# Low halves of split fp32 operands placed 128 bytes further on, modulo 256, than their high halves

## The chip, the core and the metric

The kernel runs on one core of a Trainium2 chip. Its time is the device time of one execution in microseconds (us); the figure for a kernel is the median of its runs. A profile is one further execution that the hardware profiler recorded; its span runs from the first to the last recorded instruction. TensorE (PE in the rows) does the matrix products, and its loads of the stationary operand are shown as an engine of their own, PEld. VectorE is DVE, ScalarE is ACT, GpSimd is POOL, and SP is the engine whose queue issues the DMAs.

## What is computed

Block-causal attention, then two multilayer perceptrons, all in float32 (2304 tokens, 8 heads of 64, model width 512, inner width 2048):

```python
# attention: q, k, v are (4, 8, 576, 64); query block i sees key blocks j <= i, blocks of 64
scores = np.where(mask, scale * (q @ k.T), -1e9)
x = (exp(scores - max) / (sum + 1e-9)) @ v        # -> (2304, 512)
h = x @ w1_in;  x = (h * np.cos(h)) @ w1_out      # first MLP
h = x @ w2_in;  r = np.maximum(h, 0.0)
out = (r * r) @ w2_out                            # second MLP
```

## The kernel before

**Split products.** TensorE runs the MLPs on float32 operands rounded to its short float32 form (`F32R`). To keep precision, each operand is a pair: a high half (the rounded value) and a low half (what rounding left). `hi_part` and `lo_part` make them, on ScalarE, VectorE or GpSimd. One product of pairs is three matmuls into the same PSUM bank (`mm3`, lines 903 to 907):

```python
matmul(ps, lh, rh, first, False, holds)
matmul(ps, lh, rl, False, False, holds)
matmul(ps, ll, rh, False, last, holds)
```

The first operand is stationary (128 columns, loaded into the array by an LDWEIGHTS of its own), the second one moves through it (256, 320 or 512 columns). All matmuls of this sort stand on line 548 in the profile.

**Stages.** From 0 to some 405 us the attention runs, with half of the first MLP's inner width beside it as filler for TensorE: tiles `xs1`, `xs2` (256 and 320 tokens of one batch) move through `w` into `h` banks (`h_banks`), `h * cos(h)` is split into `g` tiles (`gh0` to `gh3` high, `gl0` to `gl3` low), and these move through `w` into `y` banks (`out_T`). From 405 to 590 us the other half of the first MLP runs on blocks of 512 tokens. Its first product is done with seven block products instead of eight: `load_quarters` makes seven forms of x (`x0` to `x6`) out of sums of its quarters, `x_parts` splits each into a high and a low half in one tile (`x_tile`), and `quad` runs the seven products, 12 matmuls each, against seven forms of the weights. From 590 to 800 us the second MLP's first half runs in the same manner; its second product has g stationary and `w` moving, 512 columns. From 800 us the other half of the second MLP runs, both its products with seven forms (`g_forms`, `right_factors`, `out_quad`).

In that second-MLP stage the forms of x are also written to DRAM (`keep`, tensor `xp_d`) and read back in the last stage (`kept_parts`).

**Order.** Every operation is recorded and put into a fixed order by a planner before anything is issued; tiles get their addresses from pools that are opened one after the other. `shim` puts a few bytes between pools, so that tiles begin at chosen places.

**Places modulo 256 bytes.** In the built program every stationary `w` tile of the pool `wa` begins at 0 modulo 256, and every one of the pool `wo` at 128. Every form of x, `xs` and `g`, high and low half alike, begins at 64. In the three stages from 405 us on, the weights of the first product lie in `wo` for one half of the inner columns (`c = 0` in the stage's loop) and in `wa` for the other (`c = 1`), so TensorE goes from one place to the other where the planned order changes `c`: from `wa` to `wo` at 520.5 and 641.7 us, from `wo` to `wa` at 840.0 us. In the last stage some forms of g and of the right-hand weights take the places of other tiles (`ws`, `t`, `c`, `n`, `x`, `raw`, `so`): there both operands of a product can begin at 64 modulo 128. In the attention's scores `kh` begins at 0 and `kl` at 128; the tiles `tail` begin at 0. The slice of 288 columns (1152 bytes) that their second product takes moves each start on by 128.

Of the kernel before, what the change touches and what calls it, by code (L numbers as in the profile page):

```python
# [2 lines left out]

# [8 lines left out]
F32R = mybir.dt.float32r  # L12
# [6 lines left out]
PSUM = bass.MemoryType.PSUM  # L19
# [37 lines left out]
class View:  # L57
    def __init__(self, vt, chain, ix, halves):
        self.vt, self.chain, self.ix, self.halves = vt, chain, ix, halves
# [34 lines left out]


class VTile(View):
    def __init__(self, pool, shape, dtype, tag, bufs, whole=False):
        self.pool, self.shape, self.dtype, self.tag, self.bufs = pool, shape, dtype, tag, bufs
        self.whole = whole
        n = int(np.prod(shape[1:]))  # L100
        self.grain = 32 if n >= 32 else 1
        self.full = (1 << (2 * (n // self.grain + 1))) - 1
        self.real = None
        self.users = []
        self.bank = self.banks = self.before = None
        super().__init__(self, [], np.arange(n).reshape(shape[1:]), 3)

    def alloc(self):
        if self.real is None:
            tag = self.tag if self.bank is None else f"bank{self.bank}"  # L110
            self.real = self.pool().tile(self.shape, self.dtype, tag=tag, name=self.tag, bufs=self.bufs)


class Banks:
# [30 lines left out]
class Recorder:  # L145
# [20 lines left out]
        self.kind = None  # L166
        self.phase = 0

    def tile(self, pool, shape, dtype, tag, bufs=1, whole=False):
        return VTile(pool, shape, dtype, tag, bufs, whole)  # L170

    @contextmanager
    def of(self, kind):
# [199 lines left out]
def f(v):  # L373
    return v.bitcast(F32)


def real(v):
    return v.ap() if isinstance(v, View) else v
# [3 lines left out]
def kernel(  # L382
# [18 lines left out]
    KD = DM // 128  # L401
    HALF = DFF // 256
# [5 lines left out]
    R = Recorder()  # L408


    def of(kind):
        def wrap(fn):
            def run(*args, **kw):
                with R.of(kind):
                    return fn(*args, **kw)

            return run

        return wrap
# [40 lines left out]
    def hi_part(hi, x):  # L460
        n = hi.size
        flexible(
            "hi",
            {
                "POOL": (
                    "POOL", n * 0.836 + 160,
                    lambda: nc.gpsimd.tensor_scalar(real(hi), real(x), 1.0, 1.0, op0=ALU.mult, op1=ALU.mult),  # L467
                ),
                "DVE": (
                    "DVE", n / 1.92 + 68, lambda: nc.vector.tensor_scalar(real(hi), real(x), 1.0, None, op0=ALU.mult), 2,  # L470
                ),
                "ACT": ("ACT", n / 1.2 + 92, lambda: nc.scalar.activation(real(hi), real(x), ACTF.Copy)),  # L472
            },
            [hi], [x],
        )

    def lo_part(lo, x, hi):
        n = lo.size
        if psum(x):
            return tt(lo, x, f(hi), ALU.subtract)  # L480
        flexible(
            "lo",
            {
                "POOL": (
                    "POOL", n * 2.1 + 350,
                    lambda: nc.gpsimd.tensor_tensor(real(lo), real(x), real(f(hi)), op=ALU.subtract), 1,
                ),
                "DVE": (
                    "DVE", n / 0.96 + 68,
                    lambda: nc.vector.tensor_tensor(real(lo), real(x), real(f(hi)), op=ALU.subtract), 1,  # L490
                ),
            },
            [lo], [x, hi],
        )
# [76 lines left out]
    def dma(out, in_, size, service=None):  # L571
        R.op(
            "DMA", max(400.0, size / 360.0), lambda: nc.sync.dma_start(out=real(out), in_=real(in_)), [out], [in_],
            lat=1250,
        ).service = size / 420.0 if service is None else service
# [5 lines left out]
    class Pool:  # L581


        def __init__(self, name, **kw):
            self.name, self.kw, self.pool, self.after, self.stack = name, kw, None, (), None
# [10 lines left out]
    def opened(stack, *names, **kw):  # L596
        got = []
        for n in names:
            p = Pool(n, **kw)
            p.open(stack)  # L600
            got.append(p)
        return got

    def later(names, **kw):
        return [Pool(n, **kw) for n in names]

    def shim(stack, name, n, **kw):

        if n:
            p = stack.enter_context(tc.tile_pool(name=name, bufs=1, **kw))  # L610
            p.tile([128, n // 4], F32, tag=name, name=name)
# [19 lines left out]
    shim(ctx, "shim1", 32)  # L631
    (wa_p,) = opened(ctx, "wa")
    shim(ctx, "shim2", 64)
    cv, st_p, g_p, o_p = opened(ctx, "cv", "st", "g", "o")
    shim(ctx, "shim3", 96, side="right")
    (psum_p,) = opened(ctx, "ps", space=PSUM)
    banks = Banks(8, *BANKS)
    xs_p, tmp = opened(s1, "xs1", "tmp1")
    (sb,) = opened(att, "att", side="right")

    def T(pool, shape, dtype, tag, bufs=1):
        return R.tile(pool, shape, dtype, tag, bufs, whole=pool.kw.get("space") == PSUM)

    x_d = T(dram, [KD, 128, NT], F32, "x_d")
    y1_d = T(dram, [KD, 128, NT], F32, "y1_d")
    y_d = T(dram, [KD, 128, NT], F32, "y_d")


# [27 lines left out]
    for i in range(2):  # L676
# [3 lines left out]
        whole = T(sb, [128, 128], F32, f"whole{i}")  # L680
# [531 lines left out]
    xs = {}  # L1212

    @of("split")
    def split_x(u, r):

        o, n = GROUPS[r - 1]
        if (u.b, r) not in xs:
            xs[u.b, r] = [T(xs_p, [128, KD, n], F32R, f"xs{r}{i}") for i in "hl"]
        hi, lo = xs[u.b, r]  # L1220
        hi_part(hi[:, u.p], u.xt[:, o:o + n])
        lo_part(lo[:, u.p], u.xt[:, o:o + n], hi[:, u.p])


    def new_g():
        return [[T(g_p, [128, 2, 512], F32R, f"g{i}{m}") for m in range(HALF // 2)] for i in "hl"]

    def row(g, m):
        return g[m // 2][:, m % 2]
# [1 line left out]
    def first_in(b, r):  # L1231
        g = new_g()
        in_cos(tmp, w1i, xs[b, r], g, GROUPS[r - 1][1], TOGETHER if (b, r) == (0, 1) else 1)
        return g
# [12 lines left out]
    def attend(i):  # L1247
        u = attention(i)
        for r in (1, 2) if u.part == 0 else (u.part,):
            split_x(u, r)  # L1250
# [15 lines left out]
    for group, steps in WORK:  # L1266
        R.phase = 0 if group == (0, 1) else 1 + group[0]
        g = first_in(*group)
# [4 lines left out]
        if group in ((0, 2), (1, 1)):  # L1273
            c = group[0]
            left_weights(w1_in, 2 + c, wi_d[c])
        if group in ((1, 2), (2, 1)):
            c = group[0] - 1
            staged_weights(row_chunks(w1_out, 2 + c, 3 + c), wo_d[c:c + 1])
        if group == (3, 1):
            wo_p, x3_p = later(("wo", "x3"), side="right")  # L1280
# [9 lines left out]
    def raw_rows(src, c0, n):  # L1290
# [5 lines left out]
            raw.append(t)  # L1296
        return raw

    def x_tile(j):
        return T(x3_p, [128, 2, 2, 256], F32R, f"x{j}")  # L1300

    def x_parts(forms, keep):

        ops = {}
        for j, x in forms:
            t = x_tile(j)
            hi, lo = t[:, 0], t[:, 1]
            hi_part(hi, x)
            lo_part(lo, x, hi)
            if keep is not None:  # L1310
                dma(keep[j], f(t).rearrange("p j k c -> p (j k c)"), 524288)
            ops[j] = hi, lo
        return ops

    @of("forms")
    def kept_parts(keep, which):

        ops = {}
        for j in which:
            t = x_tile(j)  # L1320
            dma(f(t).rearrange("p j k c -> p (j k c)"), keep[j], 524288)
            ops[j] = t[:, 0], t[:, 1]
        return ops

    @of("forms")
    def load_plain(src, c0, keep=None):

        x1, x2 = raw_rows(src, c0, 256)
        d = T(tmp3, [128, 2, 256], F32, "t0")
        add(d, x2, x1, ALU.subtract)  # L1330
        return x_parts(((0, x1), (1, x2), (4, d)), keep)
# [104 lines left out]
    def g_forms():  # L1436

        small = [(st_p, f"ws{i}", 1) for i in range(2)] + [(cv, "t", 2)] * 2 + [(cv, "c", 3)] * 3
        small += [(tmp3, "n", 1)] + [(tmp3, f"t{i}", 1) for i in range(4)]
        large = [(g_p, f"g{i}{m}", 1) for i in "hl" for m in range(HALF // 2)]  # L1440
        got = [{}, {}]
        for c in range(2):
            for i in (0, 3, 4, 5, 6, 1, 2):
                if small:
                    got[c][i] = [T(pool, [128, 2, 256], F32R, tag, n) for pool, tag, n in (small.pop(0), small.pop(0))]
                else:
                    pool, tag, n = large.pop(0)
                    t = T(pool, [128, 2, 2, 256], F32R, tag, n)
                    got[c][i] = [t[:, j] for j in range(2)]
        return got  # L1450
# [86 lines left out]
    for stage in range(3):  # L1537
# [4 lines left out]
        for turn_, i in enumerate(ROUNDS[stage]):  # L1542
# [3 lines left out]
            if stage < 2:  # L1546
                xs = (load_quarters if i < 4 else load_plain)(src, c0, xp_d[i] if stage and turn_ < 4 else None)
                g = new_g()
            else:
                if turn_:  # L1550
                    xs = kept_parts(xp_d[i], FIRST if i < 4 else (0, 1, 4))
                g = g_forms()
# [27 lines left out]
            if stage < 2 and 0 < turn_ < 3:  # L1580
                c = 2 * stage + turn_ - 1
# [61 lines left out]
```

## Time and profile before

| | |
|---|---|
| median of 3 runs | 973.34 us (973.02 to 973.65) |
| profiled execution, its own time | 974.84 us |
| its span | 973.0 us |
| PE busy | 951.8 us, 98% of the span, 6996 matmuls |
| PEld busy | 856.1 us, 88% |
| DVE busy | 713.8 us, 73% |
| ACT busy | 602.3 us, 62% |
| POOL busy | 208.3 us, 21% |

The granted TensorE clock (`PEclk`) stands at full speed from 72 us to the end. A matmul's recorded duration holds the way through the array and overlaps that of the next, so it says little; what a matmul costs in a stream is the time from its start to the next one's start. The chain of work that ended last gives this: a row of it that reads "10.88 PE h L548 x96" is 96 matmuls in a row that together moved the chain on by 10.88 us, 113.3 ns each.

### The profile page before, as it was taken

Reading aid. Unit: us, or ns where it says so; the run is one execution under the profiler, and the core shown is the slowest. Engines: PE = TensorE matmul, PEld = TensorE weight load, DVE = VectorE, ACT = ScalarE, POOL = GpSimd, SP = SyncE. Lnnn points to the kernel's source line nnn. Section 1 sums busy time; section 2 is a strip of 40 time slices with the busy share of each in tenths; the row PEclk is TensorE's granted clock in tenths of the full one; section 3 lists DMA queues with packets and bytes.
Section 4 is the critical chain, followed back from the end, with each engine's and each line's share of the span. In section 5 each row is a group of like instructions: output and inputs, shape, how many; then the busy total and the mean of one; then the engine's idle time right before and its main releaser. Section 6 shows DMA issues by size and latency. Waiting matters only on the chain.

```text
span 973.0 us, 19283 instructions
## 1 busy us (share of the span) xinstructions
PE 951.8 (98%) x6996; PEld 856.1 (88%) x6996; DVE 713.8 (73%) x1581; ACT 602.3 (62%) x1285; POOL 208.3 (21%) x313
## 2 busy tenths in 40 slices
PE   7979999999999999999999999999999999999998
PEld 5757987889898989999989889998898899999998
DVE  5898667687877455588879797987885737659565
ACT  5787588785889575484758476767564433324222
POOL 3554243447687781000000000000000000000000
PEclk8999999999999999999999999999999999999999
DMA  6755233355656347563355899796947779535321
GB/s 184 192 150 124 67 85 84 105 153 182 176 174 206 109 134 263 200 254 93 109 173 181 317 360 327 268 352 215 358 139 240 245 256 416 194 104 195 96 73 60
DMA packets 155150, 185.29 MB, mean 190 GB/s; under 512 B 71728, under 2 KB 119856, under 8 KB 155056
## 3 DMA queue, kind: packets, MB, share of 16 engines
q1 hardware_dynamic: 155056, 184.07, 57.5%
q8 instruction: 55, 0.90, 0.4%
q14 instruction: 39, 0.32, 0.1%
HBM read 114.29 MB, written 69.73 MB: 189 GB/s over the span
## 4 chain that ended last, share of the span: by engine, by line
PE 88%; DMA 5%; DVE 3%; ACT 2%; issue 1%; POOL 1%; SPq 0%; ACTq 0%; POOLq 0%; DVEq 0%
PE y L548 37%; PE h L548 34%; PE t L566 6%; PE a L558 5%; PE s L558 4%; DMA wi_d<-so 2%; PE s L548 1%; DMA x<-xp_d 1%; DMA w<-wf_d 1%; DMA x<-x_d 1%; DVE e L1046 1%; POOL e L531 0%; DVE c L449 0%; DVE c L748 0%; DVE so L490 0%
## 5 line engine op out<-in xcount | busy, mean ns | idle before, releaser
L548 PE MATMUL h<-x,w 128*128 128x256 f32 x2304 | 315.8, 278 | 1.7 <-DVE r L442 0.9
L548 PEld LDWEIGHTS h<-x,w 128*128 128x128 f32 x2304 | 294.4, 188 | 6.5 <-DVE r L442 1.7
L548 PE MATMUL y<-gh,w 128*128 128x256 f32 (+2 forms) x832 | 214.7, 329 | 7.3 <-POOL w L467 6.6
L548 PEld LDWEIGHTS y<-gh,w 128*128 128x128 f32 x832 | 144.3, 189 | 19.0 <-POOL w L467 7.6
L548 PE MATMUL y<-gl,w 128*128 128x256 f32 (+2 forms) x416 | 135.0, 328 | 0.0
L548 PE MATMUL y<-w,gh 128*128 128x512 f32 (+1 forms) x450 | 124.0, 354 | 0.4 <-DVE gh L490 0.4
L548 PEld LDWEIGHTS y<-w,gh 128*128 128x128 f32 x450 | 78.9, 188 | 12.6 <-DVE gh L490 0.6
L433 ACT ACTIVATE e<-e,st 128x256 f32<-128x256 f32 (+4 forms) x144 | 82.9, 577 | 8.6 <-DVE st L1046 6.9
L1046 DVE CUSTOM_DVE_ANT_0 e<-s,mask 128x128 f32<-128x128 f32 (+4 forms) x160 | 71.3, 478 | 22.9 <-PE s L558 15.3
L531 POOL TENSOR_SCALAR e<-e,st 128x256 f32<-128x256 f32 (+4 forms) x116 | 73.0, 640 | 63.0 <-DVE st L1067 37.0
L548 PEld LDWEIGHTS y<-gl,w 128*128 128x128 f32 x416 | 78.5, 189 | 6.2 <-issue 0.8
L548 PE MATMUL y<-w,gl 128*128 128x256 f32 (+1 forms) x306 | 83.5, 333 | 0.0
L472 ACT ACTIVATE gh<-r 128x512 fp32r<-128x512 f32 (+1 forms) x85 | 51.3, 610 | 40.0 <-DVE r L1404 18.2
L566 PE MATMUL t<-ident,e 128*128 128x128 f32 (+1 forms) x400 | 65.1, 282 | 4.6 <-DVE e L535 2.3
L490 DVE TENSOR_TENSOR gl<-r,gh 128x512 fp32r<-128x512 f32 (+1 forms) x83 | 54.7, 664 | 15.3 <-ACT gh L472 12.4
L442 DVE TENSOR_TENSOR o<-y,o 128x512 f32<-128x512 f32 (+1 forms) x55 | 34.8, 635 | 40.2 <-PE y L548 39.1
L548 PE MATMUL h<-xs2h,w 128*128 128x320 f32 x256 | 62.0, 313 | 0.0
L566 PEld LDWEIGHTS t<-ident,e 128*128 128x128 f32 (+1 forms) x400 | 46.4, 141 | 13.8 <-POOL e L531 4.7
L501 ACT ACTIVATE r<-t 128x384 f32<-128x384 f32 (+1 forms) x95 | 49.2, 531 | 14.6 <-PE t L566 13.1
L433 ACT ACTIVATE t<-raw,minus 128x512 int32<-128x512 int8 x64 | 48.8, 762 | 14.8 <-DMA raw<-in_moe_w_out_dram 6.8
L548 PEld LDWEIGHTS y<-w,gl 128*128 128x128 f32 x306 | 50.2, 188 | 6.1
L548 PE MATMUL h<-xs1h,w 128*128 128x256 f32 x256 | 53.5, 290 | 1.2 <-POOL w L467 0.7
(172 smaller groups left out, 1838.0 us busy)
## 6 DMA issues: line engine op xcount, KB each, us to landing
wi_d<-so SPq DMA_DIRECT2D x84, 256.0 KB, 2.8
w<-wi_d SPq DMA_DIRECT2D x42, 512.0 KB, 6.3
raw<-in_moe_w_in_dram SPq DMA_DIRECT2D x32, 512.0 KB, 4.6
raw<-in_moe_w_out_dram SPq DMA_DIRECT2D x32, 512.0 KB, 4.4
xp_d<-x SPq DMA_DIRECT2D x24, 512.0 KB, 6.0
x<-xp_d SPq DMA_DIRECT2D x24, 512.0 KB, 5.7
y_d<-o SPq DMA_DIRECT2D x34, 256.0 KB, 2.6
o<-y_d SPq DMA_DIRECT2D x32, 256.0 KB, 3.8
```

The lines of the kernel that those rows point to most:

```text
L433: return nc.scalar.activation(real(out), real(in_), func, **kw)
L442: out.size / 0.96 + 68, lambda: nc.vector.tensor_tensor(real(out), real(a), real(b), op=op), [out], [a, b],
L472: "ACT": ("ACT", n / 1.2 + 92, lambda: nc.scalar.activation(real(hi), real(x), ACTF.Copy)),
L490: lambda: nc.vector.tensor_tensor(real(lo), real(x), real(f(hi)), op=ALU.subtract), 1,
L501: "ACT": ("ACT", n / 1.2 + 50, lambda: nc.scalar.activation(real(out), real(ps), ACTF.Copy)),
L531: lambda: nc.gpsimd.tensor_scalar(real(out), real(x), real(s), 1.0, op0=ALU.mult, op1=ALU.mult),
L548: lambda: nc.tensor.matmul(real(ps), lhsT=real(lhsT), rhs=real(rhs), start=start, stop=stop, skip_group_check=True),
L558: nc.tensor.matmul(real(ps), lhsT=real(l), rhs=real(r), start=start, stop=stop, skip_group_check=True)
L566: lambda: nc.tensor.transpose(real(out), real(in_), real(ident)[0:rows, 0:rows]), [out], [in_, ident],
L1046: lambda: nc.vector.tensor_tensor_reduce(out=real(e), in0=real(ps), in1=real(m), scale=-1.0, scalar=BIG, op0=ALU.add, op1=ALU.min, accum_o ...
```

## The change

Three sorts of low halves are moved so that they begin 128 bytes further on, modulo 256, than their high halves; on every engine the order of instructions, and what each waits for, stays the same row for row.

- `x_tile` asks for 32 elements (128 bytes) between the high and the low half of its tile. The tile grows from 4096 to 4224 bytes, so the next tile starts at another place: `x0`, `x2`, `x3`, `x5` have their high half at 192 and their low half at 64, `x1`, `x4`, `x6` the other way round.
- `xs1l` and `xs2l` get 128 bytes ahead and behind (`skip`). The high ones are now at 192, the low ones at 64.
- The low g tiles get a pool of their own, `gl`, 128 bytes behind the end of `g`: `gh` stays at 64, `gl` is at 192.

Since the halves of a form of x are no longer adjacent, the 48 DMAs between `x` and `xp_d` (24 each way, 512 KB) take two pieces of 2 KB per partition instead of one of 4 KB. In the last stage, where forms of g and of the right-hand weights use the places of `gl`, `x`, `t` and `n`, some of these begin at 192 instead of 64, but there high and low half of one form still begin at the same place modulo 256, and what was equal modulo 128 still is.

```diff
@@ class VTile: alloc @@
+            if self.skip:
+                n, (a, b) = int(np.prod(self.shape[1:])), self.skip
+                t = self.pool().tile([self.shape[0], a + n + b], self.dtype, tag=tag, name=self.tag, bufs=self.bufs)
+                self.real = t[:, a:a + n].rearrange("p (a b) -> p a b", a=self.shape[1])
+                return
...
+            n, m = int(np.prod(self.shape[1:])), int(np.prod(self.shape[2:]))
+            t = self.pool().tile([self.shape[0], n + self.apart], self.dtype, tag=tag, name=self.tag, bufs=self.bufs)
+            a = t[:, 0:n].rearrange("p (a b c) -> p a b c", a=self.shape[1], b=self.shape[2])
+            self.real = dataclasses.replace(a, ap=[a.ap[0], [m + self.apart, self.shape[1]], *a.ap[2:]])
@@ pools @@
-    cv, st_p, g_p, o_p = opened(ctx, "cv", "st", "g", "o")
+    cv, st_p, g_p = opened(ctx, "cv", "st", "g")
+    shim(ctx, "shim5", 128)
+    gl_p, o_p = opened(ctx, "gl", "o")
@@ split_x @@
-            xs[u.b, r] = [T(xs_p, [128, KD, n], F32R, f"xs{r}{i}") for i in "hl"]
+            xs[u.b, r] = [T(xs_p, [128, KD, n], F32R, f"xs{r}{i}", skip=(32, 32) if i == "l" else ()) for i in "hl"]
@@ new_g @@
-        return [[T(g_p, [128, 2, 512], F32R, f"g{i}{m}") for m in range(HALF // 2)] for i in "hl"]
+        return [[T(gl_p if i == "l" else g_p, [128, 2, 512], F32R, f"g{i}{m}") for m in range(HALF // 2)] for i in "hl"]
@@ x_tile, x_parts, kept_parts @@
-        return T(x3_p, [128, 2, 2, 256], F32R, f"x{j}")
+        return T(x3_p, [128, 2, 2, 256], F32R, f"x{j}", 1, 32)
...
-                dma(keep[j], f(t).rearrange("p j k c -> p (j k c)"), 524288)
+                dma(by_half(keep[j]), f(t).rearrange("p j k c -> p j (k c)"), 524288)
...
-            dma(f(t).rearrange("p j k c -> p (j k c)"), keep[j], 524288)
+            dma(f(t).rearrange("p j k c -> p j (k c)"), by_half(keep[j]), 524288)
```

## Rows read from the trace of the kernel before

**Rows 1.** Busy time of each engine in three stretches, with count of instructions and clock.

```profile
72.00:405.00 333.00, 331.80 (x2610) 289.50 (x2609) 229.51 (x682) 243.52 (x601) 172.88 (x256) 1.00 0.48 143
405.00:800.00 395.00, 393.25 (x2579) 356.45 (x2578) 311.92 (x560) 247.59 (x458) 0.00 (x0) 1.00 0.71 244
800.00:973.00 173.00, 168.87 (x1442) 167.91 (x1440) 116.82 (x199) 57.35 (x101) 0.00 (x0) 1.00 0.46 166
```

**Rows 2.** Chain that ended last, runs of 256-column matmuls: start, us, what, count.

```profile
365.39 6.12 PE h L548 x52
372.57 10.95 PE y L548 x93
414.02 4.73 PE h L548 x40
...
837.59 10.88 PE h L548 x96
...
953.53 5.42 PE h L548 x46
```

**Rows 3.** The same chain, one run of 320 columns and two of 512.

```profile
109.93 7.04 PE h L548 x48
...
457.48 12.82 PE y L548 x56
...
728.96 19.36 PE y L548 x83
```

**Rows 4.** The same chain, 256 columns, last stage, operands at 64 modulo 128.

```profile
848.48 1.32 PE y L548 x11
...
852.33 1.91 PE y L548 x16
```

**Rows 5.** The same chain in short windows, on both sides of two weight changes.

```profile
519.38 1.18 PE h L548 x10
...
520.79 1.13 PE h L548 x10
...
639.16 2.47 PE h L548 x21
...
642.22 1.93 PE h L548 x17
```

**Rows 6.** PE groups by line and tile, 72 to 405 us: count, busy, mean ns.

```profile
L548 PE MATMUL y<-gh,w 128*128 128x256 f32 (+1 forms) x459 | 103.1, 302 | 0.0
L548 PE MATMUL y<-gl,w 128*128 128x256 f32 (+1 forms) x229 | 67.6, 300 | 0.0
L548 PE MATMUL h<-xs2h,w 128*128 128x320 f32 x256 | 62.0, 313 | 0.0
...
L548 PE MATMUL h<-xs1h,w 128*128 128x256 f32 x192 | 40.0, 288 | 0.0
```

**Rows 7.** PE groups by line, tile and shape, 405 to 800 us.

```profile
L548 PE MATMUL h<-x,w 128*128 128x256 f32 x1621 | 213.8, 277 | 1.4 <-DVE r L442 0.9 <-ACT p L501 0.4
L548 PE MATMUL y<-w,gh 128*128 128x512 f32 x288 | 91.9, 395 | 0.0
L548 PE MATMUL y<-gh,w 128*128 128x512 f32 x256 | 82.4, 392 | 0.4 <-ACT gh L472 0.4
...
L548 PE MATMUL y<-gh,w 128*128 128x256 f32 x64 | 15.3, 277 | 0.0
...
L548 PE MATMUL y<-gh,w 128*128 128x320 f32 x30 | 7.3, 308 | 0.0
```

**Rows 8.** PE groups, 800 to 973 us: the first product.

```profile
L548 PE MATMUL h<-x,w 128*128 128x256 f32 x686 | 102.5, 278 | 0.4 <-DMA x<-xp_d 0.2 <-DMA w<-wi_d 0.2
```

**Rows 9.** Chain in a short window, the attention's last scores (288 columns).

```profile
353.57 0.53 PE s L548 x4
```

**Rows 10.** DMA issues: count, KB each, median us to landing.

```profile
x<-xp_d SPq DMA_DIRECT2D x24, 512.0 KB, 5.7
...
x<-x_d SPq DMA_DIRECT2D x8, 512.0 KB, 5.7
```

More of the change, by code (lines that the diff above doesn't have):

```diff
@@ L1 @@
+import dataclasses
 import heapq
@@ L96, with __init__ @@
 class VTile(View):
-    def __init__(self, pool, shape, dtype, tag, bufs, whole=False):
+    def __init__(self, pool, shape, dtype, tag, bufs, whole=False, apart=0, skip=()):
         self.pool, self.shape, self.dtype, self.tag, self.bufs = pool, shape, dtype, tag, bufs
-        self.whole = whole
+        self.whole, self.apart, self.skip = whole, apart, skip
         n = int(np.prod(shape[1:]))
@@ L110, in alloc @@
             tag = self.tag if self.bank is None else f"bank{self.bank}"
-            self.real = self.pool().tile(self.shape, self.dtype, tag=tag, name=self.tag, bufs=self.bufs)
+            if self.skip:
[3 more added lines that the diff above has]
+                return
+            if not self.apart:
+                self.real = self.pool().tile(self.shape, self.dtype, tag=tag, name=self.tag, bufs=self.bufs)
+                return
+            n, m = int(np.prod(self.shape[1:])), int(np.prod(self.shape[2:]))
+            t = self.pool().tile([self.shape[0], n + self.apart], self.dtype, tag=tag, name=self.tag, bufs=self.bufs)
+            a = t[:, 0:n].rearrange("p (a b c) -> p a b c", a=self.shape[1], b=self.shape[2])
+            self.real = dataclasses.replace(a, ap=[a.ap[0], [m + self.apart, self.shape[1]], *a.ap[2:]])
 class Banks:
@@ L167, in __init__, with tile @@
         self.phase = 0
-    def tile(self, pool, shape, dtype, tag, bufs=1, whole=False):
-        return VTile(pool, shape, dtype, tag, bufs, whole)
+    def tile(self, pool, shape, dtype, tag, bufs=1, whole=False, apart=0, skip=()):
+        return VTile(pool, shape, dtype, tag, bufs, whole, apart, skip)
     @contextmanager
@@ L639, with T @@
     (sb,) = opened(att, "att", side="right")
-    def T(pool, shape, dtype, tag, bufs=1):
-        return R.tile(pool, shape, dtype, tag, bufs, whole=pool.kw.get("space") == PSUM)
+    def T(pool, shape, dtype, tag, bufs=1, apart=0, skip=()):
+        return R.tile(pool, shape, dtype, tag, bufs, pool.kw.get("space") == PSUM, apart, skip)
     x_d = T(dram, [KD, 128, NT], F32, "x_d")
@@ L1297, in raw_rows, with by_half @@
         return raw
+    def by_half(t):
+        return t.rearrange("p (j c) -> p j c", j=2)
     def x_tile(j):
-        return T(x3_p, [128, 2, 2, 256], F32R, f"x{j}")
+        return T(x3_p, [128, 2, 2, 256], F32R, f"x{j}", 1, 32)
     def x_parts(forms, keep):
@@ L1439, in g_forms @@
         small += [(tmp3, "n", 1)] + [(tmp3, f"t{i}", 1) for i in range(4)]
-        large = [(g_p, f"g{i}{m}", 1) for i in "hl" for m in range(HALF // 2)]
+        large = [(gl_p if i == "l" else g_p, f"g{i}{m}", 1) for i in "hl" for m in range(HALF // 2)]
         got = [{}, {}]
```

## The prediction, made before the changed kernel was run

> **What bounds the kernel now.** I read first the busy times by stretch, then the chain of work that ended last, then the groups by tile and shape. From 72 us on TensorE is busy for 331.8 of 333, 393.25 of 395 and 168.87 of 173 us, at a granted clock of 1.00 throughout [rows 1]. ScalarE, the next busiest, has 243.5 of the first 333 us. There are few waits to remove. Since the change leaves the order alone, it can act only through the pace at which matmuls follow each other, or by making new waits.
>
> That pace is where the reader should look. A stretch of 96 matmuls of 256 columns takes 10.88 us, 113.3 ns each. Other stretches with the same shape, the same clock and operands at the same places modulo 128 take 6.12/52, 10.95/93, 4.73/40 and 5.42/46 us: 117.7 to 118.3 ns [rows 2]. So there are two paces, 4.4 ns apart. Place modulo 256 does not separate them: weights at 128 stand in the 118 ns stretch at 414 and in the first quarter of the 113 ns one at 837.6, weights at 0 in the 118 ns stretches at 365, 372 and 953 and in the rest of the one at 837.6. Scaled from the quick pace, 320 columns should take 141.7 and 512 columns 226.7 ns; the rows give 146.7, 228.9 and 233.3 [rows 3], so those widths too run 5.0, 2.3 and 6.6 ns over.
>
> Does place matter at all? Where stationary and moving operand begin at the same place modulo 128, a matmul takes 120.0 and 119.4 ns (1.32/11, 1.91/16) [rows 4], 6.1 to 6.7 ns more than in the stretch of 96. The first stretch has both at 64; the second mixes such matmuls with others whose moving operand is at 192 and stationary one at 64. For this equality 128 bytes more or less change nothing.
>
> But 128 bytes do something to the two paces. At 520.5 us the stationary operand goes from 0 to 128 while the moving one stays at 64: 1.18/10 = 118 ns before, 1.13/10 = 113 ns after. At 641.7 us it does so again: 2.47/21 = 117.6 before, 1.93/17 = 113.5 after [rows 5]. The opposite step, at 840.0 us inside the stretch of 96, does not disturb it [rows 2]. So in these rows a step of 128 between stationary and moving operand ends the slow pace and leaves the quick one alone.
>
> The Trainium skill speaks against this. Its page "SBUF — State Buffer", section "Who interferes with whom", gives TensorE two independent read ports, one for the moving operand and one for the weight load, and says that PE never waits on anyone. The trace does not agree: by that rule 120.0 and 113.3 ns could not stand beside each other. By the rule the change is worth nothing and the time stays at 973.3 us.
>
> **The change part by part.** No instruction is added, removed or moved on any engine; SP's queue issues the same DMAs in the same places.
>
> *Steps of 128.* In every product of three, the low half that moves (`xs1l`, `xs2l`, the low x, `gl` in the first MLP) or is stationary (`gl` from 590 us on) now stands 128 from the high one. So the relation of stationary to moving operand steps by 128 twice in each three matmuls, where the kernel before has one such step in many dozens. If the steps act as in rows 5, the slow pace ends soon after it begins. What the slow pace costs now:
>
> - 405 to 800 us. There are 2579 matmuls [rows 1]. 1621 are first products of 256 columns; 288 + 256 of 512 with high halves and half as many with low ones make 816; the rest are 64 + 32 of 256 and 30 + 16 of 320 columns [rows 7]. At the quick pace these are 1717 x 113.3 + 816 x 226.7 + 46 x 141.7 ns = 386.1 us; TensorE is busy 393.25, so 7.1 us are slow pace. Of these the 432 with `w` moving have 432 x 6.6 = 2.85 us, the 384 with g moving 384 x 2.3 = 0.9 us, the 46 of 320 columns 0.2 us; 3.1 us are left for the 1621.
> - 72 to 405 us. 256 + 128 matmuls of `xs2` at 5.0 ns, 192 + 96 of `xs1` at 4.4 ns and 459 + 229 of g, of both widths, at some 4.7 ns over [rows 6]: 1.9 + 1.3 + 3.2 = 6.4 us if all are slow, which both stretches of `xs1` and g in rows 2 and the one in rows 3 say.
> - 800 to 973 us. 1442 x 113.3 = 163.4 us against 168.87 busy: 5.5 us over. But the second product here keeps both halves of a form at one place modulo 256, and pairs equal modulo 128 stay equal, so it gains nothing. The 686 first products [rows 8] are already at the quick pace in the three long stretches like that of 96; the slow one at the end has 46 x 4.4 ns = 0.2 us. I put 0.3 us here.
>
> What I take of it: of the 3.1 us of first products 2.4, since rows 5 are just this case and some matmuls pass before the pace changes. Of the 3.75 us of 512 columns 1.5, since no stretch of that width shows the quick pace, so that a step might not lead to it; the bounds are 0 and 3.75. Of the 6.4 us beside the attention 3.2: the bounds are 0, if TensorE then waits instead for the attention's chain through DVE, ACT and POOL (busy for 69%, 73% and 52% of that stretch), and 6.4, if these have the slack. Sum: 2.4 + 1.5 + 3.2 + 0.3 = 7.4 us.
>
> *DMAs.* 48 transfers go in pieces of 2 KB rather than 4 KB. A load of the same 512 KB that already goes in pieces of 2 KB, `x` from `x_d`, lands in 5.7 us, as does `x` from `xp_d` [rows 10]. So nothing, at the median. The products of one block hide the loads for the next: TensorE waits 0.2 us for them in all [rows 8]. If that cover were gone at the first block of the last stage, seven loads that each land later would show at its start; I allow 0.1 us and up to 1 us in the range.
>
> *Elementwise work* gets other addresses and no other lengths. I take nothing: the engines it runs on have at least 83 of 395 us free in the busier stretch (DVE 311.9).
>
> The sum against its own execution: 974.84 - 7.4 + 0.1 = 967.5 us. That execution stands 1.5 us above the median of the runs, so for a median: 973.34 - 7.3 = **966.0 us**.
>
> **The rivals.**
>
> *Nothing changes* (973.4 us). What matters could be the place modulo 128 alone, which the change keeps, and the changes of pace at 520.5 and 641.7 us come from the change of weight tile, not from its place. For: rows 4, where 64 and 192 cost the same, and the two paces at either place in rows 2. Against: the change of tile at 840.0 us and the others inside the stretch of 96 leave the pace as it is, while both steps in rows 5 end the slow one at once. The Trainium skill's rule of independent ports ends here too.
>
> *Slower, because a constant alternation is not one step.* Rows 5 show a step and then dozens of matmuls without one. If each alternation costs something and no quick pace can settle, every affected matmul pays. The only alternation of 128 in the trace is in the last scores, where the moving operand goes 0, 128, 0 over a stationary one at 0: four matmuls of 288 columns take 0.53 us, 132.5 ns [rows 9], against 127.5 scaled from the quick pace, 5.0 ns over. There the operands are equal modulo 128 as well, so the 5.0 ns need not be the alternation's. If it were, the affected 1360 + 2579 + 686 matmuls would pay 23.1 us, against 6.4 + 7.1 + about 0.5 = 14.0 now: 9 us more, 982 us. It decides from 14.0/4625 = 3.0 ns per matmul on.
>
> *Faster by all of it.* If every affected matmul runs at the quick pace and the attention's chain gives way, the gain is 6.4 + 7.1 + 0.5 = 14 us, 959.5 us. This is the end of the forecast's own range rather than another mechanism. Its other end is a pace between the two, such as the 2.3 ns over of g moving: then 4625 x 2.3 = 10.6 us stay of 14.0, and the gain is 3.4 us, 970 us.
>
> **How the numbers follow.** Forecast, with its own range of 959.5 to 970.5: 0.58. Nothing (within 0.2%, 971.4 to 975.3, about what a measurement of this kernel can tell from no change): 0.25. Slower: 0.17, most of it below 982. The likeliest gives 966.0. For 8 in 10 I take 960 to 975.5: it holds nearly all of the forecast and the case of no change, and leaves out the slower case and the outermost gain. Faster 0.58, same 0.25, slower 0.17.
>
> **What the profile after would show.** If the steps act: in the chain, runs of `h` and `y` of 256 columns at 113 to 114 ns also between 72 and 420 us, where rows 2 have 117.7; runs of 320 near 142; the run of 512 columns with `w` moving under 233. If modulo 128 is all: the same two paces in similar shares. If alternation costs: 115 to 120 ns for 256 columns where it is 113 now, as in the three stretches of 96 after 837 us. The term for 72 to 405 us is wrong if that pace falls and idle time of TensorE for DVE, ACT or POOL grows as much. The DMA term is wrong if TensorE's wait for `x` from `xp_d` after 800 us goes well beyond 0.2 us. The whole is wrong if a step of 128 works only once, or only where it comes with a new tile.

## The result and the profile after

The changed kernel took 979.61 us (978.79 to 981.25, 6 runs) against 973.33 us (973.02 to 974.60, 6 runs) before: ratio 1.0065, 95% interval 1.0052 to 1.0078. It is slower by 6.3 us where 7.3 us less were forecast. The profiled execution took 981.25 us, its span is 979.4 us.

Busy time by stretch (PE, PEld, DVE, ACT, POOL with counts, clock, DMA share, GB/s), after:

```profile
72.00:405.00 333.00, 331.81 (x2608) 289.24 (x2606) 228.11 (x682) 243.34 (x602) 172.50 (x255) 1.00 0.48 144
405.00:800.00 395.00, 392.65 (x2530) 355.83 (x2530) 308.56 (x554) 245.42 (x454) 0.00 (x0) 1.00 0.70 240
800.00:979.00 179.00, 175.16 (x1483) 174.39 (x1482) 120.45 (x203) 59.18 (x105) 0.00 (x0) 1.00 0.48 167
```

The first stretch is as in [rows 1]. In the second, TensorE gets through 49 matmuls fewer in 395 us at the same granted clock of 1.00: it is as busy and slower. The chain after (start, us, what, count) says at which widths:

```profile
108.86 6.99 PE h L562 x48
...
364.41 6.12 PE h L562 x52
371.60 10.95 PE y L562 x93
...
457.31 12.93 PE y L562 x56
...
711.09 15.50 PE h L562 x132
...
733.84 19.24 PE y L562 x83
...
842.52 11.27 PE h L562 x96
...
959.98 5.42 PE h L562 x46
```

and the one row of the chain of before that [rows 2] do not show:

```profile
706.71 15.01 PE h L548 x132
```

Against [rows 2, 3]: beside the attention next to nothing moved, 6.12 and 10.95 us to the digit and 6.99 for 7.04. The 512-column runs went from 12.82 to 12.93 and from 19.36 to 19.24. The first products lost: the stretch of 96 from 113.3 to 117.4 ns, the one of 132 from 113.7 to 117.4. The starts give the places. Up to 365 us the new kernel is 1.0 us ahead, its granted clock from 20 to 40 us being 1.00 on average where it was 0.93; at 457 us it is 0.2 ahead, at 729 behind by 4.9 (733.84 - 728.96), at 838 by 4.9, at 954 by 6.5. One wait grew, the first of these; it was 0.4 us before [rows 7]:

```profile
PE y L562 <- ACT gh L486: 1.7, 1, 1.7
PE h L562 <- DVE r L456: 0.6, 1, 0.6
PE h L562 <- DMA x<-xp_d: 0.5, 1, 0.5
```

The trace's start times give the whole of it. I take each matmul's distance to the next start, subtract 113.3 ns scaled by its width, leave out as waits those that are 25 ns or more over, and add up the rest. By this measure the first products from 405 us on lie 3.7 us over the quick pace before and 9.9 us after. That is the loss. The pace itself shows in every four first products in a row that have no wait among them: their mean is under 115.5 ns, halfway between the two paces, in 1315 of 1776 cases before (74%) and in 3 of 1783 after. The quick pace is gone.

### The profile page after: what moved, and what is told of

The parts are those of the page before. It is cut to its first block, busy times and chain, and to the rows that moved or that the text cites. A ratio compares the mean times of both kernels' runs of the same rounds, so it can differ in the third digit from the quotient of the medians.

```text
span 979.4 us, 19283 instructions
## 1 busy us (share of the span) xinstructions
PE 956.4 (98%) x6996; PEld 861.8 (88%) x6996; DVE 713.4 (73%) x1581; ACT 602.9 (62%) x1285; POOL 209.2 (21%) x313
## 4 chain that ended last, share of the span: by engine, by line
PE 86%; DMA 6%; DVE 4%; ACT 2%; POOL 1%; issue 1%; SPq 0%; ACTq 0%; POOLq 0%; DVEq 0%
PE y L562 35%; PE h L562 35%; PE t L580 6%; PE a L572 5%; PE s L572 4%; DMA wi_d<-so 2%; PE s L562 1%; DMA x<-xp_d 1%; DMA wf_d<-so 1%; DMA w<-wf_d 1%; DMA raw<-in_moe_w_out_dram 1%; DVE e L1062 1%; DMA w<-wi_d 1%; DVE c L764 1%; DVE c L463 1%
## 5 line engine op out<-in xcount | busy, mean ns | idle before, releaser
L562 PE MATMUL h<-x,w 128*128 128x256 f32 x2304 | 321.7, 280 | 1.1 <-DVE r L456 0.6
L562 PEld LDWEIGHTS h<-x,w 128*128 128x128 f32 x2304 | 299.9, 188 | 5.6 <-DVE r L456 1.3
```

The costliest lines, as they stand in the source:

```text
L562: lambda: nc.tensor.matmul(real(ps), lhsT=real(lhsT), rhs=real(rhs), start=start, stop=stop, skip_group_check=True),
```

## The experiments

All kernels keep the order of instructions on the compute engines, except the one of streams. Beside the time, the table has three stretches of the chain: 132 first products at some 707 us, 96 first products at some 838 us (the quick pace gives 14.96 and 10.88 us) and 83 products of 512 columns at some 730 us. Times of before on the same chips: medians 973.98 to 974.57 us.

| kernel | median, us | ratio, 95% interval | x132 | x96 | x83 |
|---|---|---|---|---|---|
| before | | | 15.01 | 10.88 | 19.36 |
| after | 979.61 | 1.0065 [1.0052, 1.0078] | 15.50 | 11.27 | 19.24 |
| x_only | 980.66 | 1.0061 [1.0044, 1.0078] | 15.50 | 11.27 | 19.35 |
| g_xs_only | 977.01 | 1.0027 [1.0012, 1.0041] | 15.56 | 10.88 | 19.24 |
| pieces_only | 973.83 | 0.9997 [0.9985, 1.0009] | 15.12 | 10.88 | 19.35 |
| x_by_form | 978.29 | 1.0038 [1.0023, 1.0053] | 15.50 | 11.22 | 19.36 |
| x_and_w | 979.91 | 1.0055 [1.0043, 1.0067] | 15.59 | 11.28 | 19.36 |
| w_only | 976.73 | 1.0023 [1.0012, 1.0034] | 15.03 | 10.97 | 19.36 |
| wo_by_form | 974.71 | 1.0005 [0.9995, 1.0015] | 15.14 | 10.94 | 19.36 |
| wa_pairs | 974.12 | 1.0001 [0.9990, 1.0011] | 15.13 | 10.91 | 19.14 |
| x_at_192 | 977.82 | 1.0036 [1.0023, 1.0049] | 15.45 | 11.31 | 19.36 |
| all_at_192 | 974.76 | 1.0002 [0.9991, 1.0013] | 15.45 | 10.98 | 19.02 |
| g_by_stage | 974.33 | 1.0002 [0.9987, 1.0016] | 15.56 | 10.88 | 19.22 |
| g_on_w | 973.60 | 0.9996 [0.9982, 1.0010] | 15.56 | 10.88 | 18.86 |
| g_at_0 | 977.45 | 1.0031 [1.0018, 1.0044] | 15.56 | 11.31 | 18.86 |
| g_at_0_wo | 976.16 | 1.0019 [1.0007, 1.0031] | 15.41 | 10.94 | 18.86 |

### The parts of the change

**x_only** keeps the change of `x_tile` and its DMAs; **g_xs_only** keeps that of `xs` and `gl`; **pieces_only** has all places as before, with the transfers in two pieces. Its main line leaves a gap in the DRAM tensors:

```diff
-    xp_d = [[T(dram, [128, 1024], F32, f"xp_d{c}{i}") for i in range(7)] for c in range(5)]
+    xp_d = [[T(dram, [128, 2, 544], F32, f"xp_d{c}{i}") for i in range(7)] for c in range(5)]
```

> Only the forms of x have their low half 128 bytes on (and their DMAs go in 2 KB pieces); xs and g stay as before. Theory 1 (the step of 128 between stationary and moving operand in every product of three keeps the first products off the 113.3 ns pace): nearly the whole loss, 5.5 to 6.5 us slower than before, stretches of 96 first products in the last stage at 117 to 118 ns. Theory 2 (the loss comes from DMAs in smaller pieces landing later): slower too, but with more idle time of TensorE and stretches of 96 at 113.3 ns. Theory 3 (xs and g are what costs): within 1 us of before.

> Only xs and g are changed, forms of x and their DMAs as before. Theory 1: within 1 us of before, since the stretches beside the attention ran at 117.7 ns already and the 512-column stretches changed by plus 0.6 and minus 0.5 us in the changed kernel; first products at 113.3 ns in the stretches of 96. Theory 3: 5 us or more slower.

> All places in SBUF as before; the tensors xp_d get a gap of 128 bytes in DRAM between their halves, so that the 48 DMAs of the x forms go in 2 KB pieces as in the changed kernel. Theory 1: within 0.7 us of before. Theory 2: 3 us or more slower, with idle time of TensorE before the products that wait for DMAs or for their buffers.

The pieces cost nothing. The forms of x alone cost as much as the whole change, with the wait for `gh` at 0.4 us as before, so that wait is not the cause; of the first products 7 in 1793 cases of four are quick. `xs` and `gl` cost 0.3% by themselves, a miss for every expectation: x stands as before, yet the 132 first products behind second products with `gl` apart run at 117.9 ns. By the start times the first products lie 7.1 us over the quick pace where it was 3.7, and 2.0 of these 3.4 us come between 590 and 800 us, where only stationary halves were moved. So what the second products do changes the pace of the first products behind them. Which of their steps does it stayed open, and the rule found below, that steps of the stationary operand leave the quick pace alone, does not give it.

**x_by_form** leaves both halves of a form together and moves whole forms, so the moving operand steps every 12 matmuls:

```diff
-        return T(x3_p, [128, 2, 2, 256], F32R, f"x{j}")
+        return T(x3_p, [128, 2, 2, 256], F32R, f"x{j}", 1, 32)   # 32 elements behind the tile
```

> Each tile of a form of x grows by 128 bytes at its end, its halves stay adjacent: x0, x2, x3, x5 begin at 192 with both halves, x1, x4, x6 at 64 with both. A step of 128 comes with a change of form, every 12 matmuls, not within a product. Theory 1, with what the rows of before showed of single steps (they end the slow pace and leave the quick one alone): first products at 113 to 114 ns in more stretches than before, 1 to 3 us faster than before. If 192 itself were bad for the forms at it: half the loss, 3 us slower. If steps of 128 are without effect: as before.

The forecast's rule in its mildest form, and it failed: 0.4% slower. The chain of this kernel in short windows, all over one weight pool at 0:

```profile
721.01 0.57 PE h L554 x5
...
721.92 1.18 PE h L554 x10
...
847.00 1.26 PE h L554 x11
...
848.49 1.29 PE h L554 x11
```

At 721.6 us TensorE goes from `x0` (192) to `x1` (64): 114 ns before, 118 after. At 847.07 it goes from `x1` (64) to `x5` (192): 117.8 ns before by the start times, then 1.26/11 = 114.5 in the mean, falling to 113.3 within five matmuls. At 848.44 it is back at 64, on `x4`: 117.3. So steps of the moving operand, unlike those of [rows 5], can end the quick pace; the one at 847.07, the other way, ended a slow one.

### Which operand steps

**x_and_w** puts three forms of x and the weights of `c = 0` apart:

```diff
+        if n == 7:
+            return T(pool, [128, 2, 2, 256], F32R, "w", n, 32).rearrange("p j k c -> p j (k c)")
...
-        return T(x3_p, [128, 2, 2, 256], F32R, f"x{j}")
+        return T(x3_p, [128, 2, 2, 256], F32R, f"x{j}", 1, 32 if j in (0, 1, 5) else 0)
```

> Places are modulo 256. In three of the seven forms of x the low half lies 128 on from the high one; in the weights of one half of the inner columns (c = 0, pool wo) the low half lies 128 on from the high one. So from 405 us on the first products fall into four sorts: both operands step in each product of three, only the stationary one, only the moving one, or none. Nothing else is moved, and the transfers go in pieces of 2 KB. Theory M (a step of the moving operand in every product ends the quick pace, whatever the stationary operand does): some 117 to 118 ns for both sorts in which x steps, some 113 ns for the sort in which only the weights step. Theory P (what counts is where the moving operand of one matmul lies against the weights that are loaded while it runs): where both step the relation is constant, so 113 ns; where only the weights step 117 to 118 ns, as where only x steps. Time: by M 2 to 4 us more than before; by P 3 to 5 us more.

From the start times, waits left out: both step 118.7 ns, only the weights 117.8, only x 117.6, neither 117.0. By these means nothing is told apart, except that theory P falls; the sorts alternate every dozen matmuls and hand their pace on. Against the expectation other things moved too: the larger tiles put `x1`, `x3` and `x6` at 192, so that x also steps between forms. The share of products of three whose mean is under 115.5 ns does tell the operands apart: 1% where both step and 4% where only x does, 18% where only the weights do and 18% where neither does. What the means left open was then measured by itself.

**streams** leaves the kernel's work out and runs TensorE alone. `run` issues so many matmuls, of 256 columns or the width given; `products` gives the places of moving and stationary operand in each three of them:

```python
def products(rh, rl, lh, ll):
    return lambda i: ((rh, lh), (rl, lh), (rh, ll))[i % 3]
...
    ("sa", products(64, 64, 0, 0)),
    ("sb", products(64, 64, 128, 128)),
...
        for name, places in SORTS[1:]:
            run("x" + name[1:], places, 96)
        for name, places in SORTS[1:]:
            run("kick", products(192, 192, 0, 0), 24)
            run("y" + name[1:], places, 96)
        for name, places in SORTS[1:]:
            run("kick", products(64, 64, 0, 0), 24)
            run("step", products(64, 64, 128, 128), 24)
            run("z" + name[1:], places, 96)
        for name, places in SORTS[1:]:
            run("v" + name[1:], places, 48, 512)
```

> The kernel's own work is left out; TensorE alone multiplies short-form float32 operands, in streams of 96 matmuls of 256 columns (48 of 512 in the last set), products of three, two high and low halves in separate places, no other engine busy. Sorts, moving/stationary place modulo 256: a, c, e, g, i, k, n 64/0; b 64/128; d 192/0; f the moving one steps in every product (192, 64, 192 over 0); h the stationary one steps in every product (128, 128, 0 under 64); j both; l the stationary one steps every 12; m the moving one every 12; o 64/64; p 0/0. Theory M (a step of the moving operand ends the quick pace; one of the stationary operand does not): f, j and m at 117 to 118 ns, h and l at 113 to 114 ns, o and p at 119 to 120, the constant ones at whichever pace the stream before left. Theory N (any frequent step costs): f, h and j alike at 117 to 118. Theory T (the paces need the traffic of other engines on the memory): 113 ns in all but o and p, or in all.

Its chain, set x in a row, then pieces of sets y, z and v:

```profile
44.71 11.30 PE xa L85 x96
56.01 10.90 PE xb L85 x96
66.91 10.88 PE xc L85 x96
77.79 11.31 PE xd L85 x96
89.10 11.31 PE xe L85 x96
100.41 11.31 PE xf L85 x96
111.71 11.31 PE xg L85 x96
123.02 10.90 PE xh L85 x96
133.92 10.88 PE xi L85 x96
144.80 11.30 PE xj L85 x96
156.10 11.31 PE xk L85 x96
167.41 11.04 PE xl L85 x96
178.46 11.12 PE xm L85 x96
...
200.88 11.52 PE xo L85 x96
...
268.76 10.88 PE yd L85 x96
...
516.41 2.83 PE step L85 x24
...
533.37 2.72 PE step L85 x24
536.09 11.31 PE zf L85 x96
...
566.55 2.72 PE step L85 x24
569.27 10.88 PE zh L85 x96
...
714.15 11.20 PE va L85 x48
...
736.55 11.00 PE vc L85 x48
...
769.73 11.10 PE vf L85 x48
...
869.28 10.90 PE vo L85 x48
```

Theory M holds, but for m (115.8 ns, below the 117 expected) and l (115.0 in sets x and y, over the 114 expected), at a granted clock of 1.00 (2.4 GHz) with every other engine idle, so no traffic of others is needed. In set x the streams a, c, e, g, i and k have the same places, 64 over 0, and take 113.3 or 117.8 ns: whatever the stream before left. One step of the stationary operand (a to b) ends the slow pace, the step back (c) leaves the quick one, one step of the moving operand (c to d) ends it. Not every step from 0 to 128 ends the slow pace: the one at 516.41 us left it at 2.83/24 = 117.9 ns, and in l, by the start times, only the third step of the stationary operand did it. The start times explain m: after its first three blocks of 12 matmuls, those with the moving operand at 192 took 113.8 to 113.9 ns each and those at 64 took 117.7 to 117.8. So a step of the moving operand is no loss as such. From 64 to 192 it ended the slow pace there, the step back ended the quick one. Stepping stationary halves (h) run at 113.5 and 113.3 ns; stepping moving ones (f) at 117.8 even straight after 2.72/24 = 113.3 (the last step and zf); both together (j) at 117.7. Equal places (o) take 120.0, as in [rows 4]. The rule of the Trainium skill that the forecast set against the trace ("SBUF — State Buffer", section "Who interferes with whom": two independent read ports, PE waits on no one) does not agree with these rows either: with no other engine busy, the places of TensorE's own two operands to each other alone make 113.3 or 120.0 ns.

**w_only** does h in the kernel: x_and_w's line on the weights without that on x.

> Only the weights of one half of the inner columns (c = 0, from 405 us on) have their low half 128 on from the high one, modulo 256: of the 1621 + 686 first products, half have a stationary operand that steps in every product of three. x, xs and g are as before. Theory M (only steps of the moving operand end the quick pace): within 1 us of before, first products of c = 0 at 113 to 114 ns for most of the time. Theory N (any frequent step costs): 3 to 5 us slower, first products of c = 0 at 117 to 118 ns and half of the others too, since the pace lasts.

The stretches keep their pace, 15.03 and 10.97 us, and 69% of the cases of four first products are quick, for 74% before, so N falls. But the kernel is 0.2% slower, 2.4 us, more than M allows. By the start times the first products lie 4.5 us over the quick pace for 3.7, and the second ones of the last stage 3.3 for 3.0; TensorE waits 1.8 us for ScalarE from 405 us on, where it was 0.8 [rows 7], but less for others, so that all its waits there come to 2.8 us for 2.5. That makes 1.4 us; the rest was not settled.

**wo_by_form** and **wa_pairs** make steps of the stationary operand, to end slow paces; in wa_pairs the moving operand steps too where `w` moves, from 590 us on:

```diff
+        return T(pool, [128, 2, 512], F32R, "w", n, 32 if n == 7 else 0)   # wo_by_form
...
+            if getattr(pool, "twin", None) is not None:                     # wa_pairs: second pool 128 on
+                pool, bufs = (pool, pool.twin)[self.nth // 2 % 2], bufs // 2
```

> Each weight tile of the pool wo begins 128 on from the last one, so that the stationary operand steps by 128 modulo 256 every 12 matmuls while c = 0; x has both halves at one place (192). The moving operand never steps. Theory M (steps of the stationary operand end the slow pace and never the quick one; those of the moving one end the quick one): the first products run at the quick pace for more of the time, 1 to 2 us faster than before. Theory N (any frequent step costs, whichever operand makes it): 1 to 3 us slower, first products of c = 0 at 117 to 118 ns. Theory Z (the paces come and go without regard to places): within 1 us.

> The weight tiles of the pool wa are put at 0 and at 128 modulo 256 in turns of two, so that the stationary operand steps by 128 every 12 to 24 matmuls in the attention and in the MLPs; where w moves (512 columns, second MLP), the moving operand steps as often. x and g stay where they were. Theory M: first products and the products of g in the first MLP come out of the slow pace sooner, 2 to 4 us faster up to 590 us, and where w moves up to 1 us slower, so 1 to 4 us faster in all. Theory N (any frequent step costs): 2 to 5 us slower. Theory Z: within 1 us.

Neither gains. In wo_by_form, where x stands at 64 in the program as built and not at 192 as expected, a step from 0 to 128 ends a slow pace in 7 of 9 cases (a mean over 116 ns in the four matmuls before, under it from the fifth after), yet second products bring it in again. In wa_pairs the products beside the attention lie 4.7 us over the quick pace for 6.2 before. But TensorE then waits 1.3 us there for `gh` from ScalarE, where it did not before, and later 1.3 us for x from `xp_d`, where it was 0.2 [rows 8]:

```profile
PE y L552 <- ACT gh L476: 1.3, 1, 1.3
...
PE h L552 <- DMA x<-xp_d: 1.3, 1, 1.3
```

Over the kernel before and these six in which single steps can be found (pieces_only, g_xs_only, x_by_form, wo_by_form, wa_pairs, x_at_192), by the same measure: a step of the stationary operand met the quick pace 121 times and ended it once; one of the moving operand met it 19 times and ended it 19 times, nearly always going from 192 to 64. The slow pace was ended by 46 of 76 steps that take the distance from stationary to moving place from 64 to 192, by either operand, and by 1 of 33 that take it back.

### Place or step

**x_at_192** has x at 192, both halves; **all_at_192** has `xs` and g there too:

```diff
-                    shim(stack, "shim4", 64, side="right")
+                    shim(stack, "shim4", 192, side="right")
...
+    shim(ctx, "shim5", 128)   # all_at_192 only: ahead of the pools g, o, xs1
```

> All forms of x begin at 192 instead of 64 modulo 256, both halves; no step is added. Theories M, N and Z: within 1 us of before, the first products at 113 ns for most of the time from 405 us on, since the place itself makes no difference. If place matters after all (192 over 0 slower than 64 over 0): up to 4 us slower, with every stretch of first products over weights at 0 at 117 to 118 ns.

> x, xs1, xs2 and g, high and low halves alike, begin at 192 instead of 64, so that the moving operand steps neither within a product nor where TensorE goes from first products to second ones, as it did with x alone at 192. The weights stay at 0 and 128. Theory M: within 1 us of before. If a place of 192 itself, or a distance of 192 rather than 64 over weights at 0, is what was slow with x at 192: 3 to 5 us slower.

x at 192 alone cost 0.4% where I expected nothing: with g left at 64, the moving operand steps at every change between first and second products up to 590 us, which I had overlooked. With all of them at 192 the time is back, but the first products are not: their 132 still take 15.45 us, and by the start times those from 405 us on lie 5.8 us over the quick pace, for 7.5 with x alone at 192 and 3.7 before. The time comes back in part beside the attention (1.0 us less over) and where `w` moves at 512 columns (1.5 us less). Nor can the steps between g and x be the whole cost of x at 192: its first products lost most from 590 to 800 us (3.0 for 1.1 us), where `w` at 0 moves in between. So these two kernels do not part place from step. Two other figures do. With x at 192 throughout, 33% and 49% of the cases of four first products are quick, against 3 and 7 cases in all where x steps within each product. And in the streams 192 over 0 ran at 10.88/96 = 113.3 ns (yd) and at 11.31/96 = 117.8 (xd). The place does not fix the pace; the step in every product keeps the quick one out.

### A version that might beat both

In the streams 512 columns were at their best with both operands at one place: 10.90/48 in the row of vo, 226.7 ns by the start times once the change-over is past. **g_by_stage** puts the stationary g of 590 to 800 us at 0 and 128 in turn under `w` at 0, **g_on_w** all of them at 0, **g_at_0** every g at 0 in all stages, **g_at_0_wo** adds wo_by_form. The lines of g_on_w:

```diff
+    def g_place(tag, stage):
+        odd = tag in ("gl0", "gl1", "gh3", "gl3")
+        return ((16, 0), (0, 48))[odd][stage], (16, 48)[odd]
...
+    def new_g(stage=0):
+        tags = [[f"g{i}{m}" for m in range(HALF // 2)] for i in "hl"]
+        return [[T(g_p, [128, 2, 512], F32R, t, 1, g_place(t, min(stage, 1))) for t in ts] for ts in tags]
```

> Only the g tiles of the second MLP's first half (590 to 800 us) are moved, by 64 bytes: they are stationary there under w of 512 columns, and now begin at the same place modulo 128 as w. Everything else begins where it does in the kernel before. In the streams of TensorE alone, 512 columns at equal places took 226.7 ns, against 228.8 to 233.3 elsewhere; here the 432 matmuls of this sort are 6.3 ns over 226.7 on average. If that carries over to the kernel: 226.7 to 227 ns in these runs, 2 to 3 us faster than before (ratio 0.997 to 0.998). If equality costs here what it costs at 256 columns, 6 ns: no faster, or slower. If TensorE's stretch is given back to waits for ScalarE or a DMA later: the runs at 226.7 ns, and the time less than 1 us shorter.

> In the second MLP's first half (590 to 800 us) every g tile begins at 0 modulo 256, as w does that moves over it; elsewhere all begins as in the kernel before. Theory E (at 512 columns what counts is the same place modulo 256): the 432 products take some 227 ns, 5.5 to 6.3 ns less than before, 2.4 to 2.7 us, and the time falls by that if the first products behind them keep their 114.4 ns (113.3 + 1.1), and by nothing if those go to 117 ns (820 by 2.5 ns, 2.1 us), as they did with half of the g tiles moved. Rival: it was the alternation of g tiles and not their place, then some 232 ns and no change.

> All g tiles begin at 0 modulo 256 in every stage, x and xs at 64 as before, weights at 0 and 128 as before. Theory E: 227 ns for all 816 products of 512 columns, 2.4 to 3.7 us less; 120.0 ns for the second products of 256 columns beside the attention (315 by 2.3 ns, 0.7 us more) and for some 180 more in the last stage (by some 3 ns, 0.5 us more); 320 columns not known. Together 1 to 2.5 us faster, if the steps of 64 bytes of the moving operand between g and x do nothing to the first products. If these end the quick pace as steps of 128 do: 2 to 4 us slower, first products at 117 ns from 405 to 590 us.

> As the kernel with all g tiles at 0, and the weight tiles of wo in turns at 128 and 0, so that the stationary operand of the first products steps every 12 matmuls while c = 0. If such steps end a slow pace that the second products leave behind: 0.5 to 2 us faster than the kernel with g at 0 alone, first products under 115 ns. If they do nothing: the same time as that.

The chain of g_on_w:

```profile
705.55 15.56 PE h L554 x132
728.37 18.86 PE y L554 x83
747.23 15.63 PE h L554 x132
```

Theory E holds: 18.86/83 = 227.2 ns, 6.0 less than in [rows 3], 1.9 us over the 432 by the start times. In g_by_stage a product with g at the place of `w` took 227.6 ns when one of its own sort followed, and one with g 128 further on 232.7, so at this width the place counts modulo 256. But the first products between, untouched, went from 15.01 to 15.56 us; by the start times those of that stage lost some 2 us. What one sort gains the next gives back: 0.9996. In g_at_0 the first products come out slow in the last stage too (11.31), the second ones of 256 columns beside the attention run at 119.5 ns for 117.8, and the gain of 512 columns is overtaken; in g_at_0_wo the stationary steps bring the stretch of 96 back to 10.94. No version beats the kernel before by more than its interval.

## Why the prediction was wrong

**The step that failed** is the reading of [rows 5], "So in these rows a step of 128 between stationary and moving operand ends the slow pace and leaves the quick one alone", carried to "the relation of stationary to moving operand steps by 128 twice in each three matmuls". Both steps in those rows are of the stationary operand, single, and in one direction. They are not the only ones: the weights of the first products change place 53 times from 405 us on, and not just at the three times that the section on places names; 24 of these steps stand clear of others in the trace of before, and they say the same: 20 met the quick pace and left it, 4 from 0 to 128 ended a slow one. The change makes steps of the moving operand, up to 590 us in all its products, and in every first product after. Stream h shows the forecast's rule right for the operand that rows 5 show, stream f shows it wrong for the one that the change moves: a step of the moving operand in every product holds TensorE at 117.8 ns.

**First products, 405 to 800 us** (-2.4 us) and **last stage** (-0.3): opposite in sign. With a step in every product no quick pace can last, so those that had it lost it: from 3.7 to 9.9 us over, +6.1 before rounding.

**Beside the attention** (-3.2): nothing. `xs` and g were at 117.7 ns already, and stepping moving halves run at just that (117.8 in stream f); no slack of other engines was tried.

**512 columns** (-1.5, bounds 0 and 3.75): by the start times +0.6 for g moving and -0.5 for `w` moving, together nothing. Stream f takes 231.3 ns at this width, between the 229.2 and 233.3 of constant places.

**DMAs** (+0.1): right. pieces_only is 0.9997, and the wait for x from `xp_d` 0.5 us in place of 0.2 [rows 8].

**The rival that won** is "a constant alternation is not one step". Its mechanism was right, its price was not: it took 5.0 ns for each of 4625 matmuls from [rows 9] and reached 982 us. The step costs some 4.1 to 4.4 ns and only those that were at the quick pace. It deserved more than the 0.17 for all that is slower, since at 256 columns the profile held no 128-byte step of the moving operand, but for those in the last stage into, out of or between places equal modulo 128.

## What to carry to other kernels

A rule read from single events is a rule for those events: which operand, which direction and how often belong to it. Where a pace can be one of two and is handed on from product to product, a gain in one sort has to be weighed with the sorts behind it; g_on_w made 432 matmuls 4.4 ns shorter on average and gave it all back. When a kernel's sorts interleave too closely to be told apart, a stream of TensorE alone tells in one run.

## What was not expected of the hardware

Short-form float32 matmuls of 256 columns, back to back at a granted clock of 1.00, have two paces with the same operands at the same places, 113.3 and 117.8 ns. Either held through the 96 matmuls of a stream, and the quick one, from 450.59 us on in set z, through 456 with steps of the stationary operand alone. At 512 columns there are 226.7 ns (one place modulo 256), 228.8 and 233.3, by the start times of the streams. Equal places are the slowest case at 256 columns (120.0) and the quickest at 512. What in TensorE or its reads makes the two paces was not found, nor why stationary halves apart in one sort of product slowed the next (g_xs_only).
